# First DFT on rows that are not normalized: factors in its matrix, means as a bias of the copies

## The chip, the cores and the metric

The kernel runs on one core of one Trainium2 chip. The metric is device time of one launch in microseconds; three runs of the kernel before took 1415.65 (median), 1414.65 and 1416.2 us. A profiled execution stands beside them. The engines of the core are named as the profile names them: PE (matrix products; PEld is its loading of stationary matrices), DVE (vector), ACT (scalar engine, with activation functions), POOL (GpSimd) and SP (it issues DMA transfers; ACT and POOL can issue them too). A "q" behind an engine's name (SPq, ACTq) marks its instruction queue, which is where DMA issues show.

## The reference, cut to what matters

An adaptive layer norm, a Fourier block (AFNO) and a gated feed-forward block over 4096 rows of 640 channels:

```python
mod = (_silu(c) @ w_mod).reshape(c.shape[0], 6, 1, -1)
sa, ca, ga, sb, cb, gb = (mod[:, 0], ..., mod[:, 5])
h = _layernorm(x, axis=-1) * (1 + ca) + sa
x = x + ga * _A_ref(h, A_w1, A_b1, A_w2, A_b2)
h = _layernorm(x, axis=-1) * (1 + cb) + sb
x = x + gb * _B_ref(h, B_w_gate, B_w_up, B_w_down)
```

`_A_ref` takes the real FFT over the 4096 rows, multiplies each frequency by two block-diagonal complex layers (4 blocks of 160 channels: `w1`, `b1`, ReLU, then `w2`, `b2`), soft-thresholds at 0.01, and transforms back. `_B_ref` is the gated product `(silu(x w_gate) * (x w_up)) w_down`. Everything is computed in float32, or in pairs of a high and a low part.

## The kernel before, in words

The change touches the first 75 us or so. All of it is one function, `body`, in which each engine's instructions stand in the order in which the code writes them (`tc.manual_schedule()`).

**Stage A.** The 4096 rows are seen as 128 x 32: row n1*32 + n2. Eight tiles `xa0` to `xa7` (in the code `xas[t]`) hold 128 partitions (n1) times 4 values of n2 times 640 channels. For each tile: `ln_stats(t)` takes mean and variance on DVE (BN_STATS, BN_AGGR) and forms on POOL the factor `rs` = (var + eps)^-0.5 and the bias `nm` = -mean * rs; `ln_apply(t)` normalizes the four rows of 640 in place, some on ACT (`Identity` with scale and bias), some on DVE; `dft_a(t)` multiplies by the 128 x 128 DFT matrix `fa`: four products of 512 columns, and a fifth that gathers the last 32 channels of each block of all four rows; `evac_a(t)` copies the five results back over the tile (ACT, for the last two tiles partly DVE); `moves(t)` issues DMA transfers on SP: writes of quarters of the tile to four scratch arrays `s1` in DRAM (`write_s1`), and loads for later (`raws` are the raw weights, `wm1` a block of `w_mod` of 1600 KB).

**Between A and B.** `first_scale`, `remainders` and `columns` make `ca1`, the 1 + ca of the modulation, from `wm1` and silu(c). `weights_high` and `weights_low` split the weights of the first layer, `prep1` (12 jobs), and those of the second, `prep2` (6 jobs), into high and low parts. The second bias `b2` is loaded into one row of a zeroed tile, spread to 128 partitions by three PE products with ones, and copied to `b2t` by ACT. `idle(n)` issues n products whose result nobody uses.

**Stage B and on.** `gs[0]` (called g) holds the spectrum of the first of eight chunks. It is filled by `load_g(0, ...)` from the scratch array s10, which tiles 0 to 5 wrote, and, for tiles 6 and 7, by `move_g`, a copy of 16 rows from the tile straight into four partitions of g (40 KB, four copies per tile). `stage_b` multiplies g by a table; `evac_b` and `evac_r` copy out with the factor `ca1` and split into high (ACT) and low (DVE) parts; `stage_l1` and `stage_l2` are the two layers, for 32 positions (8 chunks times 4 blocks). From there PE works through the rest of the program in a fixed order.

**What orders the DMA issues.** Each transfer that SP or ACT issues carries one of eight semaphores, DMAHW0 to DMAHW7, shared by both engines, and is issued only when the transfer that held the same semaphore before has landed. SP issues in order: an issue that waits holds back all that stand behind it.

Of the kernel before, what the change touches and what calls it, by code (L numbers as in the profile page):

```python
# [6 lines left out]
F32 = mybir.dt.float32  # L7
# [166 lines left out]
def body(tc, x, w1, b1, w2, b2, wg, wu, wd, c, wm, k_fa, k_tb, k_tx, k_bm, k_bx, k_ga, k_ge, k_id, out, dbg=None):  # L174
# [27 lines left out]
    with ExitStack() as top:  # L202
# [35 lines left out]
        with ExitStack() as af:  # L238
# [50 lines left out]
            af.enter_context(tc.manual_schedule())  # L289
            nc.sync.dma_start(fa, k_fa)  # L290
# [45 lines left out]
            stx = ExitStack()  # L336
            xp = stx.enter_context(tc.tile_pool(name="xp", bufs=1, side="right"))
            rp = af.enter_context(tc.tile_pool(name="rp", bufs=1))
            b2t = rp.tile([P, 2, NB, BS], F32, name="b2t")
            with tc.tile_pool(name="sp", bufs=1) as sp:  # L340
                xas = []
                xts = {t: xp.tile([P, 4, D], F32, name=f"xa{t}") for t in (1, 2, 3, 0, 4, 5, 6, 7)}

                def load_x(t):
                    xa = xts[t]
                    if t < 3:
                        for i in range(4):
                            nc.sync.dma_start(xa[:, i, :], xv[:, 4 * t + i, :])
                    else:
                        nc.sync.dma_start(xa, xv[:, 4 * t:4 * t + 4, :])  # L350
                    xas.append(xa)


                def write_s1(t, f):
                    nc.sync.dma_start(s1[f][4 * t:4 * t + 4].rearrange("n r d -> r n d"),
                                      xas[t][(slice(0, 64, 4), slice(64, P, 4), slice(2, P, 4), slice(1, P, 2))[f]])

                for t in range(6):
                    load_x(t)
                wm1 = sp.tile([P, 5, D], F32, name="wm1")  # L360
                stats = {}
                pas = {}
                raws = {}


                def moves(t):
                    if t < 6:
                        write_s1(t, 0)
                    if t < 4:
                        write_s1(t, 1)  # L370
                    if t == 0:
                        load_x(6)
                        nc.sync.dma_start(c5, c)
                    elif t == 1:
                        load_x(7)
                        raws[1] = load_weights(sp, w1, "1")
                    elif t == 2:
                        nc.sync.dma_start(wm1, wm[:, 1])
                    elif t == 3:
                        load_tb(0)  # L380
                        nc.sync.dma_start(b1m, b1[:, 0:8].rearrange("p (r b) -> p r b", r=2))
                        nc.sync.dma_start(b1r, b1[0:64, 8:12])
                        nc.sync.dma_start(b2s[0:1], b2.rearrange("r b o -> (r b o)").unsqueeze(0))
                    elif t == 4:

                        load_g(0, (0, 1))
                        raws[2] = load_weights(rp, w2, "2", (0,))
                    elif t == 5:
                        for f in (2, 3):
                            write_s1(1, f)  # L390
                    elif t == 6:

                        for i in range(4):
                            move_g(0, t, i, (pool, nc.sync)[i // 2])
                        load_g(0, (2,))
                    elif t == 7:
                        for i in range(4):
                            move_g(0, t, i, (pool, nc.sync)[i // 2])


                def ln_stats(t):
                    n = 1 if t < 2 else 4
                    for i in range(0, 4, n):
                        mv, rs = layer_stats(lp, xas[t][:, i:i + n, :], n, f"a{t}_{i}")
                        nm = lp.tile([P, 4], F32, tag="nm", bufs=7, name=f"nm{t}_{i}")
                        pool.tensor_tensor(nm[:, :n], mv[:, :, 0], rs, op=OP.mult)
                        pool.tensor_tensor(nm[:, :n], nm[:, :n], mone[:, :n], op=OP.mult)
                        for k in range(n):
                            stats[t, i + k] = (mv[:, k, 0:1], rs[:, k:k + 1], nm[:, k:k + 1])

                def ln_apply(t):
                    xa = xas[t]
                    for i in range(4):
                        mean, rs, nm = stats[t, i]
                        if i >= (4, 2, 2, 3, 2, 3, 2, 1)[t]:
                            dve.tensor_scalar(xa[:, i, :], xa[:, i, :], mean, rs, op0=OP.subtract, op1=OP.mult)
                        else:
                            act.activation(xa[:, i, :], xa[:, i, :], AF.Identity, bias=nm, scale=rs)


                b2s = sp.tile([P, 2 * NB * BS], F32, name="b2s")
                pool.memset(b2s, 0.0)
                acc0 = sp.tile([P, D], F32, name="acc0")
                wx0 = sp.tile([P, P], F32, name="wx0")

                def first_scale(lo, hi):
                    if lo == 0:
                        dve.tensor_scalar(acc0, wm1[:, 0, :], sc[:, 0:1], None, op0=OP.mult)
                    for k in range(max(lo, 1), hi):
                        dve.scalar_tensor_tensor(acc0, wm1[:, k, :], sc[:, k:k + 1], acc0, op0=OP.mult, op1=OP.add)  # L430

                def dft_a(t):

                    xnr = xas[t].rearrange("p a (b e) -> p a b e", b=NB)
                    for n, i in enumerate((0, 1, 2, 3, 4) if t < 7 else (4, 0, 1, 2, 3)):
                        j = 5 * t + n
                        pa = (bank0(j // 4, [P, 512], f"pa{t}_{i}") if j % 4 == 0
                              else ps.tile([P, 512], F32, tag=f"p{j % 4}", name=f"pa{t}_{i}"))
                        mm(pa, fa, xnr[:, i, :, 0:128] if i < 4 else xnr[:, :, :, 128:160], start=True, stop=True)
                        pas[t, i] = pa  # L440

                def evac_a(t):
                    xa = xas[t]
                    for i in range(5):
                        if t > 5 and i % 2:
                            dve.tensor_copy(xa[:, i, 0:512], pas[t, i])
                        elif i == 4:
                            act.activation(xa[:, :, 512:640], pas[t, i].rearrange("p (a e) -> p a e", a=4), AF.Copy)
                        else:
                            act.activation(xa[:, i, 0:512], pas[t, i], AF.Copy)  # L450

                ln_stats(0)
                ln_stats(1)
                ln_apply(0)
                for t in range(8):
                    if t + 2 < 8:
                        ln_stats(t + 2)
                    if t + 1 < 8:
                        ln_apply(t + 1)
                    dft_a(t)  # L460
                    if t == 6:

                        prep1 = prep_weights(raws[1], w1a, w1b, w1c, True)
                        for job in prep1[:6]:
                            weights_high(*job, pool)
                        first_scale(0, 2)
                    evac_a(t)
                    if t == 6:
                        first_scale(2, 5)
                        remainders(acc0, wx0)  # L470
                    if t == 2:
                        act.activation(sc, c5, AF.Silu)
                    moves(t)

                pm1 = columns(acc0, wx0)
                dve.tensor_scalar(ca1, pm1[:, 0:5], 1.0, None, op0=OP.add)

                pbs2 = []
                for n, w in enumerate((512, 512, 256)):
                    pbs2.append(ps.tile([P, 512], F32, tag="p2" if n else "p1", name=f"pb2_{n}"))  # L480
                    mm(pbs2[n][:, :w], ones, b2s[:, 512 * n:512 * n + w], start=True, stop=True)
                idle(4)
                for job in prep1[6:]:
                    weights_high(*job)
                b2v = b2t.rearrange("p r b o -> p (r b o)")
                for n, w in enumerate((512, 512, 256)):
                    act.activation(b2v[:, 512 * n:512 * n + w], pbs2[n][:, :w], AF.Copy)
                for job in prep1:
                    weights_low(*job)
# [2049 lines left out]
```

## Time and profile before

| what | us |
| --- | --- |
| three runs: median (lowest, highest) | 1415.65 (1414.65, 1416.2) |
| the profiled execution | 1411.32 |
| its span, first to last instruction | 1409.5 |
| PE busy in the span | 1382.5 (98%) |
| first product of stage A starts | 7.98 |
| first product of stage B starts | 55.84 |

The profiled execution is 4.3 us under the median of the runs. Its span is divided by the traces into instructions with a start and a duration; times below are counted from the span's start. In a row of the timeline the first number is the start, the second the time from the start of the first to the end of the last of a merged group, and "x40" the number of instructions in it. A float32 product shows as two instructions. A bracket at the row's end says how long the engine had been idle before, and what it was waiting for.

### The profile page before, as it was taken

To read this page: it belongs to the slowest core of one execution; us is meant where nothing else is said; L and a number is where in the kernel's file an instruction comes from. 1 tells how busy PE (TensorE), PEld (TensorE's weight loads), DVE (VectorE), ACT (ScalarE), POOL (GpSimd) and SP (SyncE) were. 2 spreads that over 40 slices of the span, in tenths; PEclk is the share of its full clock that TensorE was granted. 3 is DMA by queue.
4 is the path that set the end of the run, shared out by engine and by line. 5 is a ranking of instruction groups with operands and counts; after the bars stand their busy time and mean duration, and the time that the engine had idled before them with its cause. 6 is when DMAs were issued, how large, how long until landed. Compare 5 with 4: busy or idle time off the path is not lost. (4 is left out here: it accounts for less than half of the span.)

```text
span 1409.5 us, 23754 instructions
## 1 busy us (share of the span) xinstructions
PE 1382.5 (98%) x8410; PEld 1310.7 (93%) x8410; DVE 1067.8 (76%) x1861; ACT 765.0 (54%) x1542; POOL 604.6 (43%) x683
## 2 busy tenths in 40 slices
PE   6899999999999999999999999999999999999998
PEld 2599999967999889899999999999999999999998
DVE  8889888889888888649787668678678757375644
ACT  6879999755555554436454345546164624262341
POOL 5700200157766594326445534447153624042241
PEclk9999999999999999999999999999999999999999
DMA  9876466675998897898877998696998668956634
GB/s 371 310 244 211 157 196 193 203 232 170 327 353 308 308 335 263 293 368 308 308 225 281 375 330 288 236 326 230 375 330 309 217 218 282 350 194 217 199 115 149
DMA packets 171016, 377.34 MB, mean 268 GB/s; under 512 B 22193, under 2 KB 81649, under 8 KB 168882
## 3 DMA queue, kind: packets, MB, share of 16 engines
q1 hardware_dynamic: 161794, 359.28, 73.6%
q0 software_dynamic: 6800, 13.93, 3.1%
q10 hardware_dynamic: 2304, 2.62, 0.5%
q8 instruction: 66, 1.08, 0.3%
q14 instruction: 52, 0.43, 0.1%
HBM read 269.48 MB, written 96.80 MB: 260 GB/s over the span
## 5 line engine op out<-in xcount | busy, mean ns | idle before, releaser
L1442 DVE TENSOR_TENSOR wb<-r,wb 128x768 fp32r<-128x768 f32 (+3 forms) x170 | 170.4, 1013 | 13.5 <-ACT wb L1435 13.3
L2050 PE MATMUL pw<-h,wt 128*128 128x384 f32 x412 | 139.3, 338 | 0.6 <-ACT s_y L2069 0.6
L2052 PE MATMUL pw<-h,wt 128*128 128x384 f32 x412 | 138.3, 336 | 0.0
L2051 PE MATMUL pw<-h,wt 128*128 128x384 f32 x412 | 138.1, 335 | 0.0
L1435 ACT ACTIVATE wb<-r 128x768 fp32r<-128x768 f32 (+3 forms) x168 | 104.5, 639 | 56.3 <-PE pw L2063 41.7
L2351 PE MATMUL pc<-wq,L 128*128 128x320 f32 x846 | 132.7, 309 | 0.9 <-DMA wq<-wqd 0.9
L2110 POOL TENSOR_TENSOR sg<-s_x,sg 128x384 f32<-128x384 f32 x24 | 30.0, 1250 | 234.5 <-DVE s_x L2076 234.5
L2351 PEld LDWEIGHTS pc<-wq,L 128*128 128x128 f32 x846 | 126.3, 188 | 1.1 <-DVE x L2308 1.1
L2130 DVE TENSOR_TENSOR L<-sg,L 128x384 fp32r<-128x384 f32 x144 | 101.0, 725 | 27.7 <-ACT L L2126 27.2
L2069 ACT ACTIVATE s_x<-pw 128x384 f32<-128x384 f32 x52 | 25.6, 492 | 164.2 <-PE pw L2052 162.3
L2050 PE MATMUL pw<-h,wb 128*128 128x384 f32 x312 | 105.0, 336 | 0.0
L2051 PE MATMUL pw<-h,wb 128*128 128x384 f32 x312 | 104.4, 335 | 0.0
L2052 PE MATMUL pw<-h,wb 128*128 128x384 f32 x312 | 104.4, 335 | 0.0
L2121 POOL TENSOR_TENSOR sg<-sg,sg 128x384 f32<-128x384 f32 x72 | 91.9, 1276 | 23.4 <-DVE L L2130 20.0
L1973 PE MATMUL pg<-ht,wb 128*128 128x512 f32 x260 | 101.8, 392 | 0.0
L2351 PE MATMUL pe<-wq,L 128*128 128x320 f32 x648 | 101.7, 309 | 0.0
L1974 PE MATMUL pg<-ht,wb 128*128 128x512 f32 x260 | 101.3, 390 | 0.0
L1975 PE MATMUL pg<-ht,wb 128*128 128x512 f32 x260 | 101.2, 389 | 0.0
L2267 PE MATMUL pd<-wq,a 128*128 128x320 f32 x632 | 96.8, 310 | 0.0
L2351 PEld LDWEIGHTS pe<-wq,L 128*128 128x128 f32 x648 | 96.6, 188 | 0.0
L2267 PEld LDWEIGHTS pd<-wq,a 128*128 128x128 f32 x632 | 93.5, 188 | 0.5
L772 POOL DMA_DIRECT2D s<-co x28 | 15.7, 559 | 175.9 <-ACT co L771 175.9
(317 smaller groups left out, 3914.1 us busy)
## 6 DMA issues: line engine op xcount, KB each, us to landing
wq<-wqd SPq DMA_DIRECT2D x83, 640.0 KB, 6.1
wt<-td SPq DMA_DIRECT2D x103, 512.0 KB, 5.4
hs<-ho SPq DMA_DIRECT2D x52, 512.0 KB, 5.2
h<-hs SPq DMA_DIRECT2D x32, 768.0 KB, 7.9
td<-wt SPq DMA_DIRECT2D x25, 512.0 KB, 6.3
r<-in_B_w_gate_dram SPq DMA_DIRECT2D x24, 384.0 KB, 4.4
r<-in_B_w_up_dram SPq DMA_DIRECT2D x24, 384.0 KB, 4.3
xx<-tt SPq DMA_DIRECT2D x56, 160.0 KB, 3.3
```

The lines of the kernel that those rows point to most:

```text
L1435: def high(ks, e=slice(0, c), copy=lambda o, i: act.activation(o, i, AF.Copy)):
L1442: dve.tensor_tensor(wbs[t, n][:, 1, ks, e], raw[t, n][:, ks, e], f32(wbs[t, n][:, 0, ks, e]), op=OP.subtract)
L1973: mm(b, wh, hh, start=(kk == 0), stop=False)
L1974: mm(b, wh, hl, start=False, stop=False)
L1975: mm(b, wl, hh, start=False, stop=(kk == 4))
L2050: mm(b, w(0, kp), a[:, kp, 0], start=start and kp == 0, stop=False, skip_group_check=not start)
L2051: mm(b, w(0, kp), a[:, kp, 1], start=False, stop=False, skip_group_check=not start)
L2052: mm(b, w(1, kp), a[:, kp, 0], start=False, stop=kp == 1, skip_group_check=not start)
L2121: pool.tensor_tensor(o, x, y, op=op)
L2130: dve.tensor_tensor(o[:, 1], raws[j], f32(o[:, 0]), op=OP.subtract)
L2267: mm(b[:, :320], l, m, start=start and i == 0, stop=stop and i == len(s) - 1)
L2351: mm(o[:, :320], ls[q][:, x, k], w[:, q, y], start=start and q == 0 and n == 0, stop=q == 1 and n == 2, skip_group_check=not start)
```

## The change

Rows of tiles 1 to 6 are no longer normalized before the DFT. Since the factor `rs` belongs to a partition (n1), over which the DFT sums, it is multiplied into a copy of the DFT matrix: `scaled` makes four matrices `wt` per tile on ACT (128 x 128 each). The means are handled apart: one small product of `fa` with the four columns of `nm` gives the transform of the means (`pa` number 5), `bias_a` copies it to `bt`, and `evac_a` adds it as a bias while it copies. The last 32 channels of each block, which share one product over all four rows, are still normalized in place (`rest`, ACT). Tile 0 is normalized on ACT and tile 7 on DVE, as rows (`ln_row`).

"Moves": tile by tile, `move_g` now brings chunk 0 into g from all eight tiles (32 copies; those of tile 7 with even number on ACT's queue, all others on SP); `write_s1(t, 0)` and `load_g(0, ...)` with data are gone. All eight loads of x stand at the start of SP's queue; c is loaded first on ACT's queue. "Second bias": `b2t` is loaded by one DMA that reads b2 once per partition. "Lower parts": `weights_low` of jobs 6 to 11 of `prep1` stand behind and between the `evac_b`/`evac_r` of the first two blocks. `idle(14)` stands ahead of tile 0, `idle(6)` replaces `idle(4)`. From stage B on each engine's order is that of before.

```diff
+            nc.scalar.dma_start(c5, c)
             nc.sync.dma_start(fa, k_fa)
...
-                for t in range(6):
+                for t in range(8):
                     load_x(t)
+                load_g(0, ())
+                act.activation(sc, c5, AF.Silu)
+                idle(14)
...
                 def moves(t):
-                    if t < 6:
-                        write_s1(t, 0)
+                    for i in range(4):
+                        move_g(0, t, i, nc.scalar if t == 7 and i % 2 == 0 else nc.sync)
                     if t < 4:
                         write_s1(t, 1)
...
                     elif t == 4:
-                        load_g(0, (0, 1))
+                        for f in (2, 3):
+                            write_s1(1, f)
                         raws[2] = load_weights(rp, w2, "2", (0,))
                     elif t == 5:
-                        for f in (2, 3):
-                            write_s1(1, f)
-                    elif t == 6:
-                        for i in range(4):
-                            move_g(0, t, i, (pool, nc.sync)[i // 2])
-                        load_g(0, (2,))
-                    elif t == 7:
-                        for i in range(4):
-                            move_g(0, t, i, (pool, nc.sync)[i // 2])
+                        nc.sync.dma_start(b2t.rearrange("p r b o -> p (r b o)"),
+                                          b2.rearrange("r b o -> (r b o)").unsqueeze(0).to_broadcast([P, 2 * NB * BS]))
...
+                def scaled(t, *rows):
+                    if t not in wts:
+                        wts[t] = sp.tile([P, 4, P], F32, tag="wt", bufs=2, name=f"wt{t}")
+                    for i in rows:
+                        act.activation(wts[t][:, i, :], fa, AF.Copy, scale=stats[t, i][1])
+
+                def rest(t, *rows):
+                    for i in rows:
+                        _, rs, nm = stats[t, i]
+                        v = xas[t][:, i, :].rearrange("p (b e) -> p b e", b=NB)[:, :, 128:160]
+                        act.activation(v, v, AF.Identity, bias=nm, scale=rs)
...
+                    for i in (4, 0, 1, 2, 3) if t == 7 else (0, 1, 2, 3, 4) if t == 0 else (0, 1, 2, 3, 5, 4):
+                        pa = pas[t, i] = bank_a(f"pa{t}_{i}")
+                        if i == 5:
+                            mm(pa[:, 0:4], fa, nms[t], start=True, stop=True)
+                        elif i == 4:
+                            mm(pa, fa, xnr[:, :, :, 128:160], start=True, stop=True)
+                        else:
+                            mm(pa, fa if plain else wts[t][:, i, :], xnr[:, i, :, 0:128], start=True, stop=True)
...
+                for t in range(2, 7):
+                    if t < 6:
+                        ln_stats(t + 2)
+                    scaled(t, 0, 1)
+                    bias_a(t - 1)
+                    rest(t, 0, 1)
...
+                    scaled(t, 2, 3)
+                    evac_a(t - 1, *((2, 3) if t == 2 else (0, 1, 2, 3)))
+                    rest(t, 2, 3)
+                    evac_a(t - 1, 4)
+                    dft_a(t)
+                    moves(t - 1)
+                prep1 = prep_weights(raws[1], w1a, w1b, w1c, True)
+                for job in prep1[:6]:
+                    weights_high(*job, pool)
+                first_scale(0, 1)
+                for i in range(4):
+                    ln_row(7, i)
+                first_scale(1, 2)
+                bias_a(6)
+                evac_a(6, 0, 1, 2, 3, 4)
+                dft_a(7)
+                moves(6)
...
+                evac_a(7, 0, 1, 2, 3, 4)
+                moves(7)
...
-                for n, w in enumerate((512, 512, 256)):
-                    act.activation(b2v[:, 512 * n:512 * n + w], pbs2[n][:, :w], AF.Copy)
-                for job in prep1:
+                for job in prep1[:6]:
                     weights_low(*job)
...
+                weights_low(*prep1[6])
+                evac_b(0, 0)
+                evac_r(0, 0)
+                for job in prep1[7:]:
+                    weights_low(*job)
```

**How instructions stand now: SP.** The names are those of the tiles with a running number behind (`xa3_118` is tile 3, `xa7_123` tile 7), and the brackets name the semaphores that an issue waits for. Before, behind tile 4's write to s10, SP loads parts 0 and 1 of g, and the first copies into g are those of tiles 6 and 7:

```order
L355 DMA s10<-xa4_119 16x4x640 [waits DMAHW2_49,DVE_49,Activation_49]
L311 DMA g0_453<-s10 32x2560 [waits DMAHW3_49]
L311 DMA g0_453<-s10 32x2560 [waits DMAHW4_49]
L253 DMA rm2_456<-in_A_w2_dram 128x1280 [waits DMAHW5_49]
L355 DMA s10<-xa5_120 16x4x640 [waits DMAHW6_49,DVE_49,Activation_49]
```

Now copies of tiles 3 and 4 stand there:

```order
L317 DMA g0_141<-xa3_118 4x4x640 [waits DMAHW5_49,Activation_49]
L317 DMA g0_141<-xa3_118 4x4x640 [waits DMAHW6_49]
L317 DMA g0_141<-xa3_118 4x4x640 [waits DMAHW7_49]
L317 DMA g0_141<-xa3_118 4x4x640 [waits DMAHW1_49]
L416 DMA s11<-xa3_118 16x4x640 [waits DMAHW3_49]
L299 DMA tb0_519<-in_k_tb_dram 128x512 [waits DMAHW4_49]
L444 DMA b1m_81<-in_A_b1_dram 128x8 [waits DMAHW5_49]
L445 DMA b1r_82<-in_A_b1_dram 64x4 [waits DMAHW6_49]
L317 DMA g0_141<-xa4_120 4x4x640 [waits DMAHW7_49,Activation_49]
L317 DMA g0_141<-xa4_120 4x4x640 [waits DMAHW0_49]
L317 DMA g0_141<-xa4_120 4x4x640 [waits DMAHW1_49]
L317 DMA g0_141<-xa4_120 4x4x640 [waits DMAHW2_49]
```

The semaphores go round in turn, 5, 6, 7, but in the fourth and fifth row SP goes on with 1 and 3: 0 and 2 of this round belong to the two transfers of ACT shown next. Behind these rows SP still has, in order, two writes to s1, `rm2`, four copies of tile 5, `b2t`, four of tile 6 and two of tile 7.

**ACT.** Around the end of stage A, before:

```order
L448 ACTIVATE xa6_121<-pa6_4_513 128x4x128 [waits DVE_49,Activation_49]
L450 ACTIVATE xa7_122<-pa7_0_539 128x512 [waits PE_49,Activation_49]
L450 ACTIVATE xa7_122<-pa7_2_543 128x512 [waits DVE_49,PE_49]
L448 ACTIVATE xa7_122<-pa7_4_537 128x4x128 [waits PE_49]
L283 ACTIVATE w1a_92<-rm1_320 128x4x128 [waits DMAHW7_49]
```

Now, with two of the copies of tile 7 behind its last evacuation:

```order
L533 ACTIVATE xa7_123<-pa7_2_640 128x512 [waits PE_49]
L525 ACTIVATE xa7_123<-pa7_4_634 128x4x128 [waits DVE_49,PE_49]
L317 DMA g0_141<-xa7_123 4x4x640 [waits DMAHW0_49,Activation_49]
L317 DMA g0_141<-xa7_123 4x4x640 [waits DMAHW2_49]
L283 ACTIVATE w1a_92<-rm1_394 128x4x128 [waits DMAHW5_49]
```

The two copies are the transfers of this round that hold DMAHW0 and DMAHW2.

**DVE.** Ahead of tile 7's DFT, before:

```order
L416 TENSOR_SCALAR xa6_121<-xa6_121,mv_a6_0_414,rs_a6_0_427 128x640
L416 TENSOR_SCALAR xa7_122<-xa7_122,mv_a7_0_460,rs_a7_0_473 128x640 [waits DVE_49,Pool_49]
L416 TENSOR_SCALAR xa7_122<-xa7_122,mv_a7_0_460,rs_a7_0_473 128x640 [waits DVE_49] x2
L428 TENSOR_SCALAR acc0_141<-wm1_138,sc_67 128x640 [waits DMAHW3_49,Activation_49]
L430 SCALAR_TENSOR_TENSOR acc0_141<-wm1_138,sc_67,acc0_141 128x640 [waits DVE_49]
```

And now:

```order
L495 TENSOR_SCALAR acc0_159<-wm1_158,sc_67 128x640 [waits DMAHW4_49,Activation_49]
L476 TENSOR_SCALAR xa7_123<-xa7_123,mv_a7_0_524,rs_a7_0_531 128x640 [waits Pool_49]
L476 TENSOR_SCALAR xa7_123<-xa7_123,mv_a7_0_524,rs_a7_0_531 128x640
L476 TENSOR_SCALAR xa7_123<-xa7_123,mv_a7_2_535,rs_a7_2_542 128x640 [waits DVE_49,Pool_49]
L476 TENSOR_SCALAR xa7_123<-xa7_123,mv_a7_2_535,rs_a7_2_542 128x640 [waits DVE_49]
L497 SCALAR_TENSOR_TENSOR acc0_159<-wm1_158,sc_67,acc0_159 128x640 [waits DVE_49]
```

The first multiplication with `wm1`, which waits for that load, moved from behind the rows of tile 7 to ahead of them.

More of the change, by code (lines that the diff above doesn't have):

```diff
@@ L624, in evac_rh @@
                 if b == 0:
[L625 removed]
+                    rzs[ch] = lp.tile([P, NB, 258], F32R, tag="rz", bufs=2, name=f"rz{ch}")
                     if ch == CE:
@@ new lines, in mod_sum @@
+            def mod_sum(m, hf=0):
+                if m == 0:
+                    pm = columns(acc, wx)
+                    dve.tensor_scalar(sa4, pm[:, 0:5], float(S), None, op0=OP.mult)
+                elif m == 2:
+                    pm = ps.tile([P, 512], F32, tag="p3", name=f"pm{m}_{hf}")
+                    mm(pm[:, :320], ones, acc[:, 320 * hf:320 * hf + 320], start=True, stop=True)
+                    act.activation(gab[:, 320 * hf:320 * hf + 320], pm[:, :320], AF.Copy)
+                else:
+                    pm = ps.tile([P, 512], F32, tag="p3", name=f"pm{m}")
+                    for t in range(5):
+                        mm(pm[:, t:t + 1], acc[:, 128 * t:128 * t + 128], ones[:, 0:1], start=True, stop=True)
+                    if m == 3:
+                        dve.tensor_copy(sb1, pm[:, 0:5])
+                    else:
+                        dve.tensor_scalar(cb1, pm[:, 0:5], 1.0, None, op0=OP.add)
@@ new lines, in body @@
+            weights_rest(3)
+            weights_high(*prep2[5], pool)
+            weights_rest(5)
+            mods = {26: [(load_e,)]}
+            sums = {}
+            for i, m in enumerate((0, 2, 3, 4)):
+                for k in range(5):
+                    mods.setdefault(3 + 6 * i + k, []).append((mod_load, m, k))
+                    mods.setdefault(5 + 6 * i + k, []).append((mod_add, m, k))
+                sums.setdefault(11 + 6 * i if m < 4 else LAST, []).append((mod_sum, m, 1))
+                if m == 2:
+                    sums.setdefault(10 + 6 * i, []).append((mod_sum, m, 0))
```

393 lines of the change are left out of this document (182 added, 211 removed).

## The prediction

> **What bounds the kernel now.** I read the page first (busy shares, the span in slices), then the waits of PE by stretch, then the timeline of the head engine by engine.
>
> ```profile
> PE 1382.5 (98%) x8410; PEld 1310.7 (93%) x8410; DVE 1067.8 (76%) x1861; ACT 765.0 (54%) x1542; POOL 604.6 (43%) x683
> PE   6899999999999999999999999999999999999998
> ...
> PE py L1688 <- DMA gt<-in_k_ga_dram: 1.5, 1, 1.5
> ```
>
> PE is busy all through except in the first slices, and from 75 us to the end its longest single wait is 1.5 us (last row). So from 75 us on PE bounds, and the order there is that of before: when the head ends later by d, the end is later by d. The question is when stage B starts, and how long PE needs from there until it is dense.
>
> ```profile
> 7.98 4.64 PE L439 MATMUL pa<-xa,fa 128*128 128x512 f32 x5 [7.98 <-ACT xa L418]
> 19.60 4.82 PE L439 MATMUL pa<-xa,fa 128*128 128x512 f32 x10
> 31.56 17.74 PE L439 MATMUL pa<-xa,fa 128*128 128x512 f32 x40 [1.81 <-ACT xa L418]
> 48.48 0.60 ACT L450 ACTIVATE xa<-pa 128x512 f32<-128x512 f32 x1 [1.06 <-PE pa L439]
> 49.34 0.60 ACT L448 ACTIVATE xa<-pa 128x512 f32<-128x512 f32 x1 [0.26 <-PE pa L439]
> 50.76 1.20 SPq L316 DMA_DIRECT2D g<-xa  x2
> 55.84 2.92 PE L600 MATMUL pb<-tb,g 128*128 128x128 f32 x24 [1.43 <-DMA g<-xa]
> ```
>
> Rows 3 to 7 are the chain at the end of the head: products of stage A until 49.30, the last evacuations until 49.94, copies into g until 51.96, stage B at 55.84 after a wait for g. In stage A PE is nearly full: 40 records in 17.74 us is .427 each for the second of every pair (a product is two records, .86 us). DVE and ACT, which the change relieves, therefore hold PE by little: the gap of 1.81 us in row 3, the .71 us ahead of tile 1, and the start at 7.98. The gain to be had is a few us of 49; against it stands what the change does to SP's queue.
>
> **The change part by part.** *Work removed.* DVE normalizes 4 rows instead of 13 and ACT 4 instead of 19:
>
> ```profile
> 40.53 1.95 DVE L416 TENSOR_SCALAR xa<-xa,mv_a,rs_a 128x640 f32<-128x640 f32 x3 [0.93 <-POOL rs_a L198]
> 34.61 2.55 ACT L418 ACTIVATE xa<-xa,nm,rs_a 128x640 f32<-128x640 f32 x3
> 51.39 0.30 ACT L283 ACTIVATE w1a<-rm 128x128 fp32r<-128x128 f32 x1
> 51.59 0.30 ACT L283 ACTIVATE w1b<-rm 128x128 fp32r<-128x128 f32 x1
> 51.13 2.40 PE L481 MATMUL pb<-b2s,ones 128*128 128x512 f32 x6
> 53.13 0.87 ACT L487 ACTIVATE b2t<-pb 128x512 f32<-128x512 f32 x2 [0.26 <-PE pb L481]
> 29.19 1.28 ACT L472 ACT_TABLE_LOAD   x1
> ```
>
> On DVE 9 x .65 (1.95/3) = 5.9 us go; on ACT 15 x .85 (2.55/3) = 12.8 us, and 1.28 for a table load. ACT gets 24 `scaled`, 24 `rest` and 6 `bias_a`: the 128x128 copies start .20 apart, so 54 x .20 = 10.8. The second bias loses 2.40 on PE, .87 and another half of it on ACT; its broadcast DMA adds 640 KB. The six products with `nm` are at most .20 each. PE gets 20 records of `idle(14)` and `idle(6)` together, ahead of tile 0 and behind tile 7, where it idles before anyway. All of this I cost at nothing, gains and losses, because tile 7's products and stage B will be set by other things, below. If that cover fails, the lighter engines could give back at most the 1.81 + .71 us above.
>
> *wm1 is issued later.* SP's queue now begins with all loads of x, 8 x 1.31 MB, so all have to come in at the rate seen:
>
> ```profile
> 0.00:10.00 10.00, 2.02 (x3) 0.94 (x4) 4.82 (x21) 3.12 (x3) 4.64 (x16) 1.00 0.77 246
> 10.00:20.00 10.00, 9.29 (x18) 3.63 (x17) 9.79 (x31) 6.49 (x10) 7.89 (x25) 1.00 1.04 424
> 20.00:30.00 10.00, 9.65 (x22) 3.56 (x20) 10.00 (x34) 9.67 (x16) 3.88 (x8) 1.00 1.02 419
> fa<-in_k_fa_dram SPq DMA_DIRECT2D x1, 64.0 KB, 1.9
> SPq L348 <- DMA xa<-in_A_x_dram: 1.6, 2, 1.0
> SPq L350 <- DMA xa<-in_A_x_dram: 1.4, 3, 0.5
> wm<-in_w_mod_dram SPq DMA_DIRECT2D x1, 1600.0 KB, 11.0
> ```
>
> (Last two numbers of the windows: DMA share and GB/s.) 10.49 MB are 2.46 in the first 10 us, 4.24 in the next, and the remaining 3.79 at 419 GB/s: 29.0, plus 1.9 for a landing = 31.0 for tile 7. Rows 5 and 6 show the semaphore rule at work before: SP stood 3.0 us for earlier loads of x when it issued loads into fresh tiles. SP's third copy of tile 1 has the semaphore of tile 7's load, hence goes out at 31.0. Behind it stand ten issues ahead of `wm1`:
>
> ```profile
> 25.79 0.43 SPq L253 DMA_DIRECT2D rm<-in_A_w_dram  x1
> 26.26 0.48 SPq L253 DMA_DIRECT2D rr<-in_A_w_dram  x1
> 29.20 1.18 SPq L355 DMA_DIRECT2D s<-xa  x2
> 30.43 0.58 SPq L378 DMA_DIRECT2D wm<-in_w_mod_dram  x1
> 42.40 0.97 DVE L428 TENSOR_SCALAR acc<-wm,sc 128x640 f32<-128x640 f32 x1
> ```
>
> That is 6 copies at .60 (1.20/2 above), 2 writes at .59, .43 and .48: 5.7, with the gaps 5.9, so `wm1` is issued at 36.9 instead of 30.43. It lands between 42.6 (its bytes and what is queued, 3.3 MB from 32.9 on at .42 MB/us, plus 1.9) and 47.9 (36.9 and the 11.0 of before); I take 44.0, nearer to the first, since the loads of x that filled its 11.0 us are done. Before, `first_scale` waited for this load behind tile 7's rows; now it stands ahead of them. So tile 7's rows begin at 44.0 + .97 and end 4 x .65 later: its first product starts at 47.6. Before, its ten records began about 45.0 (49.30 less ten of .427). Tile 6 is done near 42, so PE idles some 5.5 us ahead of tile 7.
>
> *Cold products.* Rows 1 and 2 of the head show two speeds of the same record: five started in 4.6 us after the idle 7.98 us, ten in 4.8 us later on. After the gap of 1.81 us there is no slow stretch. The new gap of 5.5 us lies between the two; 5.5 is nearer to 7.98, so I take the slow speed for five records: 5 x .42 = 2.1 us. (The windows show a clock of 1.00 in both stretches, so only the spacing tells.) [...] Product 2 of tile 7 is then done at 47.6 + 2.1 + 4 x .86 = 53.2, and ACT's two last evacuations of .60 end at 54.5.
>
> *SP waits for ACT.* This is the main term. ACT's two copies of tile 7 hold DMAHW0 and DMAHW2 of the round in which SP issues tile 3's copies; SP's second copy of tile 4 is the next user of DMAHW0, and stands there until ACT's copy has landed. ACT can't issue it before tile 7 is evacuated, 54.6.
>
> ```profile
> out_dram<-x ACTq DMA_DIRECT2D x12, 160.0 KB, 1.8
> g<-xa POOLq DMA_DIRECT2D x4, 40.0 KB, 5.0
> 52.01 0.44 SPq L492 DMA_DIRECT2D rr<-in_A_w_dram  x1
> ```
>
> A copy of 40 KB issued by ACT lands between 1.8 us (ACT's own writes of 160 KB at the end of the program) and 5.0 (POOL's copies of the same 40 KB in the head); with less traffic than in the head I take 2.5: 57.1. Only then SP issues, in a row: 3 copies of tile 4, two writes, `rm2`, 4 copies of tile 5, `b2t`, 4 of tile 6, 2 of tile 7. That is 13 copies at .60, 2 writes at .59, and .44 twice: 9.9; with gaps, 17 x .61 = 10.4, of which the last issue takes .6. It starts at 66.9, lands 1.8 to 5.0 later, and I take 3.5, the middle: g is whole at 70.4. Stage B waits for all of g: 70.4 instead of 55.84, +14.6. The 16 issues ahead of the last are pure SP time, as long as no landing in the round is later than its eighth successor's issue (8 x .61 = 4.9 us); landings of 5 us just fit.
>
> *Lower parts, and the start of stage B.* Jobs 6 to 11 now stand behind the first residues on DVE:
>
> ```profile
> 54.53 0.69 DVE L286 SCALAR_TENSOR_TENSOR w1b<-rm,w1b 128x512 fp32r<-128x512 f32 x1
> ...
> 56.14 0.28 DVE L286 SCALAR_TENSOR_TENSOR w1c<-rr,w1c 128x128 fp32r<-128x128 f32 x1
> 57.73 0.75 DVE L608 SCALAR_TENSOR_TENSOR z<-pb,ca,z 128x512 fp32r<-128x512 f32 x1 [1.31 <-ACT z L607]
> ```
>
> Five of them are 1.9 us (54.53 to 56.42). Before, they lay ahead of g, with 1.31 us of idle behind them; now DVE has nothing to do from about 51 to 70, and then has them on the path of `z`. Most of 1.9 is lost, up to all of it. PE comes from 14 us of idling to stage B; its first twelve products (24 records in 2.92 us, a third of them of the next group) start at the slow speed, at most 1.5 us more. Together 1.6 to 3.4, taken as 2.6: the parts overlap, as a slow PE gives DVE time.
>
> *Sum.* 14.6 + 2.6 = +17.2. Against the profiled execution of 1411.32 (span 1409.5) that is 1428.5. The median of the runs, 1415.65, lies 4.3 higher, for all of the program; the difference is added to it: 1432.9.
>
> [...] The table of DMA issues gives 6.7 us for the quarter writes of 160 KB and 5.0 for copies of 40 KB, at a full queue, so size alone can't be told from waiting. [...]
>
> **The rivals.**
> - *Copies on a quarter of the engines.* If a 40 KB copy moves at a quarter of the 424 GB/s of the windows, it takes .39 us instead of .10; if each of the last 6 waits for the one ahead, g comes 6 x .29 = 1.7 us later: 1434.6. The 5.0 us of POOL's copies speak for it, the full queue at that time against it.
> - *No slow products.* If 5.5 us of idling doesn't slow PE, 2.1 fall away at tile 7, and at stage B 1.0: 1432.9 - 3.1 = 1429.8. For it: a clock of 1.00 in every window.
> - *SP is not held by ACT's copy.* If SP goes on at 46 with tile 4 and only `wm1` is late, stage B starts about 2.6 us later (tile 7 at 47.6 instead of 45.0), and the lower parts and slow products cost up to 2.6: 1415.65 + 5.2 = 1420.8. Against it: SP did stand for landings in the two rows of waits.
> - *The other side: no wait for a semaphore's earlier holder binds at all.* Then `wm1` keeps its place behind the same bytes and lands near 40.5, tile 7 starts at 40.5 + .97 + 2.6 = 44.1 (-.9), the copies from SP land in 3.5 instead of POOL's 5.0 (-1.5), and the lower parts cost 1.6: -.8, 1414.8, within what can't be told from no change. It decides if SP's second copy of tile 4 goes out before 46 and `wm1` before 33. The same two rows speak against it.
>
> **How the numbers follow.** The forecast with slow products in both places .50; a quarter of the engines .18; no slow products .20; SP not held .04; no semaphore binds .03; something else .05, spread. About .2% (2.8 us) is what a measurement of this kernel can tell from no change. All but the fourth rival and a part of the rest are slower: slower .94, the same .04, faster .02. The time is the forecast's, 1432.9. Its unknowns are the landing of `wm1` (-1.4, +3.9), of ACT's copy (-.7, +2.5), of the last copy (-1.7, +1.5) and the start of stage B (-1.0, +.8). Added as independent, the lower side is 2.6 and the upper 5; with the rival without slow products at 1429.8 and its own spread the range reaches down to 1426.5, with the quarter of the engines up to 1438.5.
>
> **What would show it.** In the trace after: SP idle from about 46 to 57 ahead of the second copy of tile 4, released by a copy into g; then 17 issues without a gap; `wm1` landing near 44, with DVE idle ahead of the first `acc`; PE idle for 5 to 6 us ahead of tile 7's first product and for 14 us ahead of stage B, and after both gaps records at .85 instead of .43; stage B's first product near 70; from 90 us on the same rows as before, 17 us later. It is wrong if SP issues tile 4's copies as soon as tile 4 is evacuated, or if stage B starts before 62.

## The result, and the profile after

The changed kernel took 1437.97 us (median of 4 runs, 1435.35 to 1441.57), the kernel before 1415.93 (4 runs): 1.0155 of it, with a 95% interval of 1.0128 to 1.0181. It is 22 us slower; the forecast was 17.2, with a range that ended at 1438.5. The profiled execution is the lowest of the four, 1435.35, with a span of 1433.5.

The page first (busy shares and the span in slices), then the two waits of PE and of SP that carry the head, by the view of waits between 40 and 90 us (PE) and 40 and 57 us (SP):

```profile
PE 1391.0 (97%) x8448; PEld 1320.1 (92%) x8448; DVE 1059.4 (74%) x1851; ACT 769.9 (54%) x1578; POOL 597.8 (42%) x690
PE   8499999999999989999999999999999999999998
```

```profile
PE pb L351 <- DMA rr<-in_A_w_dram: 17.0, 1, 17.0
PE pa L513 <- DVE xa L476: 1.9, 1, 1.9
...
PE pl L720 <- DVE w1c L286: 1.3, 1, 1.3
```

```profile
SPq L317 <- DMA g<-xa: 8.7, 2, 8.1
SPq L299 <- DMA wm<-in_w_mod_dram: 3.5, 1, 3.5
```

PE is busy 8.5 us longer than before, most of it the added idle products and slow records; the loss is one hole, 17.0 us ahead of stage B, in the second slice. (Its wait is put down to `rr`, but stage B reads g and tb only: by the semaphore events of the trace the last copy into g landed at 72.60, .09 us ahead.) SP stands 8.1 us for the landing of a copy into g, and ahead of that 3.5 for `wm1`. The timeline of the head of PE, of DVE where `wm1` arrives, of ACT at the end of stage A, and of SP:

```profile
45.15 1.13 PE L513 MATMUL pa<-xa,fa 128*128 128x512 f32 x2 [0.67 <-ACT xa L488]
48.22 1.13 PE L513 MATMUL pa<-xa,fa 128*128 128x512 f32 x2 [1.94 <-DVE xa L476]
49.18 3.60 PE L515 MATMUL pa<-xa,fa 128*128 128x512 f32 x8
72.69 5.19 PE L351 MATMUL pb<-tb,g 128*128 128x128 f32 x24 [17.00 <-DMA rr<-in_A_w_dram]
89.57 0.60 PE L770 MATMUL pc<-w2a,h 128*128 128x320 f32 x3
```

```profile
45.52 0.55 DVE L495 TENSOR_SCALAR acc<-wm,sc 128x640 f32<-128x640 f32 x1 [9.86 <-DMA wm<-in_w_mod_dram]
```

```profile
53.44 1.75 ACTq L317 DMA_DIRECT2D g<-xa  x2
```

```profile
36.23 0.58 SPq L441 DMA_DIRECT2D wm<-in_w_mod_dram  x1
...
46.97 9.29 SPq L317 DMA_DIRECT2D g<-xa  x2
55.70 0.56 SPq L317 DMA_DIRECT2D g<-xa  x1
...
63.05 5.09 SPq L317 DMA_DIRECT2D g<-xa  x6
```

Read from the right end: ACT's copies of tile 7 go out at 53.44, as the last evacuation ends. SP's copies of tile 4 begin at 46.97; the second of them starts at 55.70, when ACT's first copy has landed (55.69 by its semaphore events). From there SP issues with short waits only until its last copy into g, the sixth of the row at 63.05, and stage B starts at 72.69. The same place in the kernel before is

```profile
70.42 0.61 PE L711 MATMUL pc<-w2a,h 128*128 128x320 f32 x3
```

so that at the second layer's first products the changed kernel is 89.57 - 70.42 = 19.15 us late, of which 16.85 were there when stage B began. At PE's last product it is 23.7, and 24.0 by the spans (1433.5 - 1409.5). The 4.6 us in which the lateness grows from 19.15 to 23.7 come at one late wait, for `gt`, and behind it, told with the experiments.

### The profile page after: what moved, and what is told of

Its sections match the earlier page's. It is cut to its first block, busy times and chain, and to the rows that moved or that the text cites. A ratio compares the mean times of both kernels' runs of the same rounds, so it can differ in the third digit from the quotient of the medians.

```text
span 1433.5 us, 23911 instructions
## 1 busy us (share of the span) xinstructions
PE 1391.0 (97%) x8448; PEld 1320.1 (92%) x8448; DVE 1059.4 (74%) x1851; ACT 769.9 (54%) x1578; POOL 597.8 (42%) x690
```

## The experiments

Each kernel was timed in five rounds beside the kernel before; ratios are to that one. The changed kernel, timed once more in this way, stands first.

**Once more.**

> The changed kernel once more, on the chip of the runs beside it: its time against the kernel before was 1.0155 (1.0128 to 1.0181), and that is expected again.

Measured 1.0167 (1.0145 to 1.0190), 1435.81 against 1413.88 us. Its profile shows what varies from execution to execution of one and the same kernel:

```profile
49.47 1.12 PE L513 MATMUL pa<-xa,fa 128*128 128x512 f32 x2 [2.92 <-DVE xa L476]
50.43 5.29 PE L515 MATMUL pa<-xa,fa 128*128 128x512 f32 x8
```

```profile
PE py L1731 <- DMA gt<-in_k_ga_dram: 1.6, 1, 1.6
```

Here the gap ahead of tile 7 was 2.92 us, and eight records took 5.29 instead of 3.60: the slow products that the profile above does not have. Stage B began at 75.23. Then again the wait for `gt`, 1.6 here (view of waits from 500 to 560 us), was 3.7 in the first profile. The two profiled executions lose nearly the same by their last product, 22.6 us here and 23.7 in the first, but at different places: here 21.7 of it was there at the second layer's first products.

**SP held by ACT's copy.** All copies of tile 7 on SP:

```diff
-                        move_g(0, t, i, nc.scalar if t == 7 and i % 2 == 0 else nc.sync)
+                        move_g(0, t, i, nc.sync)
```

> The changed kernel with all four copies of tile 7 on SP, so that no copy of ACT holds a semaphore that SP needs earlier. Theory (SP is held by ACT's copy): SP issues tile 4's second copy near 47 instead of 55.70, the issues up to tile 7's last copy run from 45.8 on, 20 of them at .65 us, the last near 59, and stage B starts at 62 instead of 72.69; the time falls by 10 to 11 us, to 1427. Rival (the late wm1 and the rows of tile 7 behind it set the end, the hold only fills the time): stage B moves by less than 2 us and the time stays at 1436 to 1438.

Measured 1.0109 (1.0083 to 1.0136); stage B at 65.27, 7.4 us earlier than in the first profile of the changed kernel.

```profile
46.35 0.57 SPq L445 DMA_DIRECT2D b1r<-in_A_b_dram  x1
47.03 2.38 SPq L317 DMA_DIRECT2D g<-xa  x4
...
55.63 6.28 SPq L317 DMA_DIRECT2D g<-xa  x8
```

All four copies of tile 4 go out from 47.03 on: the hold is gone, and it was ACT's copy. What is left ahead of them is the wait of 3.5 us for `wm1`, up to the first row shown. In time the ratio falls by .0046 to .0058, 6.5 to 8 us, where 10 to 11 were expected, and stage B begins 3 us later than expected, since SP took 14.9 us for the 20 issues from 47.03 on (.75 each), with waits of .7, .5 and .6 us for `rm2`, b2t and ACT's evacuation among them, and tile 7 fell into slow records:

```profile
49.14 2.07 PE L513 MATMUL pa<-xa,fa 128*128 128x512 f32 x2 [2.33 <-DVE xa L476]
51.01 5.39 PE L515 MATMUL pa<-xa,fa 128*128 128x512 f32 x8
...
65.27 4.34 PE L351 MATMUL pb<-tb,g 128*128 128x128 f32 x24 [6.42 <-DMA g<-xa]
```

A window of that profile has the clock beside it (after the busy times of PE, its loads, DVE, ACT and POOL; then DMA share and GB/s):

```profile
48.00:50.00 2.00, 0.86 (x1) 0.50 (x2) 2.00 (x5) 0.66 (x2) 0.00 (x0) 0.50 0.23 75
```

PE had waited .67 and 2.33 us within 4 us, and the granted clock went to .50.

**Rows of tile 7 first.** On DVE the first multiplication by `wm1` behind them:

```diff
-                first_scale(0, 1)
                 for i in range(4):
                     ln_row(7, i)
-                first_scale(1, 2)
+                first_scale(0, 2)
```

> The changed kernel with the first multiplication by wm1 behind the rows of tile 7 on DVE, as in the kernel before. Theory (wm1 delays tile 7, whose evacuation releases SP): tile 7's first product starts at 46.4, right behind tile 6, instead of 48.22, and everything behind it, SP's issues too, is 1.8 us earlier: 1436.2. Rival (the evacuations of tile 6 on ACT keep tile 7 where it is): no change, 1438.

Measured 1.0141 (1.0113 to 1.0170). Tile 7's products follow tile 6's without a gap, and stage B begins 2.7 us earlier, at 70.02:

```profile
45.06 1.98 PE L513 MATMUL pa<-xa,fa 128*128 128x512 f32 x4 [0.67 <-ACT xa L488]
```

So `wm1`, and its new place on DVE, did delay tile 7, by 2 to 3 us. In time the difference to the changed kernel lies within the intervals; the trace shows it, the ratio alone doesn't.

**PE kept at work.** `idle(60)`, then `idle(74)`, instead of `idle(6)` behind tile 7:

> The changed kernel with idle(60) in place of idle(6): PE multiplies ones until about 70 us and idles under 3 us ahead of stage B instead of 17. Theory (the slow start of stage B is PE's clock after idling): its first 24 records take 2.9 us instead of 5.19, and the time falls by 2.3 us, to 1435.7. Rival (the first products are slow because g and tb are still being written, or for another reason in the data): the 24 records keep 5.2 us and the time stays at 1438.

> The changed kernel with idle(74) in place of idle(6): at the .114 us for each record that the run with idle(60) showed, PE multiplies ones until 70.9 and stops 2 us ahead of stage B instead of 17 (in the run with idle(60) it stopped 4.7 ahead, and stage B stayed slow). Theory (the slow start of stage B is PE's clock after idling): the first 24 records of stage B take 2.9 us instead of 5.2, and the time falls by 2.3 us against the changed kernel. Rival (another reason in the data): they keep 5.2 us, the time is the same.

Measured 1.0144 (1.0117 to 1.0171) and 1.0145 (1.0127 to 1.0163). The first stopped too early, since a record took .114 us and not the .13 I had counted on:

```profile
54.73 13.64 PE L335 MATMUL pz<-ones 128*128 128x128 f32 x120
73.08 5.20 PE L351 MATMUL pb<-tb,g 128*128 128x128 f32 x24 [4.71 <-DMA s<-xa]
```

The second kept PE at work until 1.60 us ahead of stage B:

```profile
75.86 2.92 PE L351 MATMUL pb<-tb,g 128*128 128x128 f32 x24 [1.60 <-DMA g<-xa]
```

After 17.0 us of idling the 24 records took 5.19 us, after 4.71 us 5.20, after 1.60 us 2.92: here idling sets their speed, and the price is 2.3 us. It varies: 6.42 and 5.86 us of idling in the runs with all copies on SP and with the order put right gave 4.34 and 4.55. The expected fall of 2.3 us in time isn't resolved, as the intervals of both ratios overlap with those of the changed kernel, and stage B began no earlier. In the changed kernel's windows the clock is .50 ahead of that place, and 1.00 again from 78 us on:

```profile
64.00:72.00 8.00, 0.00 (x0) 0.00 (x0) 0.00 (x0) 1.36 (x2) 5.46 (x4) 0.50 0.66 206
...
78.00:80.00 2.00, 1.88 (x14) 1.51 (x13) 1.97 (x3) 1.94 (x5) 1.92 (x2) 1.00 1.09 324
```

**A late head alone.** The kernel before with `idle(68)` in place of `idle(4)`:

> The kernel before with idle(68) in place of idle(4): stage B starts at 71.3 instead of 55.84, with PE warm, and nothing else is changed. Theory (behind the head PE bounds, a shift of d in the head is d at the end): 1415.9 + 15.5 = 1431.4. Rival (a late head also lengthens the later waits of PE, which in the changed kernel grew by 4.6 us at 344 and 530 us): 1434 to 1436.

Measured 1.0076 (1.0050 to 1.0103), 1424.59 against 1411.5: 13.1 us. The idle products took .113 us a record here too, so stage B began at 68.46, 12.6 us late and not 15.5. A shift of 12.6 gave 13.1 in the medians, which looks like one to one. The profile shows that it isn't, step by step. At the second layer the lateness is 10.15 us (80.57 - 70.42), as PE's waits there for DVE (1.1 us for `r` and .7 for `z` in the kernel before) are gone:

```profile
80.57 0.60 PE L711 MATMUL pc<-w2a,h 128*128 128x320 f32 x3
```

From there it goes through whole up to the wait for `gt` (10.1 ahead of it, at 518.87 in this profile), and that wait was 1.7 us, against 1.5 before. At the end of this execution it is 15.0 (1424.5 - 1409.5): smaller waits behind 700 us added the rest. So the theory holds from the second layer to the late waits, and those vary by as much as the rival's price. That the medians agree with 12.6 is in part luck.

**The wait for gt.** POOL issues tile 0's copies, so that its loads of `gt` carry the same semaphores as before:

```diff
-                        move_g(0, t, i, nc.scalar if t == 7 and i % 2 == 0 else nc.sync)
+                        move_g(0, t, i, nc.scalar if t == 7 and i % 2 == 0 else pool if t == 0 else nc.sync)
```

> The changed kernel with the four copies of tile 0 issued by POOL instead of SP: POOL issues as many transfers in the head as in the kernel before. It tells what lengthens PE's later wait for gt (1.5 us before, 3.7 in the changed kernel, and again after idling a slow PE). Theory (gt is loaded by POOL, whose semaphores go round, and the head's four missing issues moved it to another place in the round): the wait is 1.5 us again, no slow records at 530 us, and the time falls by 3 to 4 us. Rival (gt lands late because of the traffic of SP's queue at that place): it stays at 3 to 4 us; stage B, which hangs on SP's later issues, stays at 72 to 73 by both.

Measured 1.0147 (1.0129 to 1.0166). In its profile PE waits 3.4 us for `gt`: the turn of the semaphores is not the cause. What that wait costs the first profile of the changed kernel is read from it and from the kernel before, at the same instruction:

```profile
508.62 0.38 PE L1688 MATMUL py<-chh,gt 128*128 128x320 f32 x1 [1.51 <-DMA gt<-in_k_ga_dram]
```

```profile
530.05 0.38 PE L1731 MATMUL py<-chh,gt 128*128 128x320 f32 x1 [3.74 <-DMA gt<-in_k_ga_dram]
```

The lateness is 21.43 us here (530.05 - 508.62), 2.2 of it from the wait (1.51 to 3.74), so 19.2 ahead of it, as at the second layer. Behind it slow records follow, at a granted clock of .96 between 500 and 540 us against 1.00 before, and smaller waits, up to 23.7. The long wait isn't forced by the change: an execution of the changed kernel without it exists (1.6 us, above), and of the two runs below that keep the transfers of the kernel before, one has it (3.7) and one doesn't (1.1). Between its issue and PE's use of it `gt` took 4.2 us in the kernel before, 5.9 here and 4.3 in the second profile; why, was not settled.

**The order put right.** Five moves, the new DFT kept:

```diff
+                wm1 = sp.tile([P, 5, D], F32, name="wm1")
+                nc.sync.dma_start(wm1, wm[:, 1])
                 load_g(0, ())
...
-                        move_g(0, t, i, nc.scalar if t == 7 and i % 2 == 0 else nc.sync)
+                        move_g(0, t, i, nc.sync)
...
-                        for f in (2, 3):
-                            write_s1(1, f)
...
-                first_scale(0, 1)
...
-                first_scale(1, 2)
+                first_scale(0, 2)
...
-                for job in prep1[:6]:
+                for job in prep1:
                     weights_low(*job)
```

(The load of `wm1` at its old place goes away; the writes of tile 1 and the load of b2t go behind the copies.)

> The changed kernel with five moves of issues and order: wm1 loaded right behind the x loads; all copies of tile 7 on SP; the first multiplication by wm1 behind tile 7's rows; the two writes of tile 1 and the load of b2t behind the copies into g; all lower parts ahead of stage B. Theory (the order of the issues and of DVE costs the time, not the new DFT): wm1 lands at 34, tile 7's products start at 46.4, SP's issues run from 34 on, 32 of them at .65 us, the last copy starts near 55, and stage B starts at 58 to 59; with the waits behind it as in the changed kernel the time is 1.003 to 1.006 of the kernel before. Rival (ACT, full in stage A since it scales the matrices, would keep stage B beyond 62 whatever the order): 1.009 or more.

Measured 1.0070 (1.0050 to 1.0090), where the theory had 1.003 to 1.006 and the rival 1.009 or more: about 1 percentage point comes back, 12 us between the medians of the same rounds (1435.81 and 1424.18). Tile 7 starts right behind tile 6 and SP's last copies go out one behind the other:

```profile
50.49 7.28 SPq L317 DMA_DIRECT2D g<-xa  x12
```

```profile
59.87 4.55 PE L351 MATMUL pb<-tb,g 128*128 128x128 f32 x24 [5.86 <-DMA g<-xa]
```

Stage B begins 2.1 us after the last copy ends its issue (57.77); it is SP's 32 issues, .61 each, that still end last, 4.0 us behind the kernel before. The slow records come on top (4.55 us instead of 2.92), and then waits of PE for POOL's parts of the second layer's weights (1.5, 1.2 and .8 us).

**The new DFT alone**, and with DVE helping. The loads, writes, copies, second bias, lower parts and the place of `first_scale` are those of the kernel before; then DVE takes over

```diff
-                        elif t == 6 and i % 2:
+                        elif t in (4, 5, 6) and i % 2:
                             dve.tensor_scalar(xa[:, i, 0:512], pas[t, i], bts[t][:, i:i + 1], None, op0=OP.add)
...
+                        if t == 6:
+                            dve.tensor_scalar(v, v, stats[t, i][0], rs, op0=OP.subtract, op1=OP.mult)
```

> The new DFT alone: factors in the matrix, means as a bias, and idle(14) at the start, but with the loads, writes, copies, second bias, lower parts and the place of the first multiplication by wm1 of the kernel before. Theory (ACT, at 5.54 us for a tile in the changed kernel, paces stage A, and PE's 4.7 is not reached): tile 7's first product at 46.4 against 45.0 before, stage B at 57.3 against 55.84, the time 1.001 of the kernel before. Rival (the rows taken off DVE and ACT shorten stage A by the 2.5 us that PE waited there): 0.998.

> As the run with the new DFT alone, but DVE, idle from 36 us on, copies out two of the four rows of tiles 4 and 5 (ACT's .57 us each) and normalizes the last 32 channels of tile 6 (1.54 us of ACT). Theory (ACT paces stage A): the tiles 5 to 7 follow at 4.7 us instead of 5.54, tile 7 starts near 44.5, stage B at 55.3, the time 0.999 to 1.000 of the kernel before, and 1.5 to 2 us under the run with the new DFT alone. Rival (PE or DVE paces it): no difference between the two.

Measured 1.0026 (1.0011 to 1.0040) and 1.0022 (1.0007 to 1.0036). (Both keep `idle(14)` and the early load of c.) The forecasts were 1.001, and .999 to 1.000: both times came out slower than expected. The first rival, .998, is outside the interval. In time the DFT alone costs 3 to 4 us; the other 18 or so of the 22 belong to the moves, the second bias, the lower parts and the place of `wm1`. In the head it costs less: at the second layer's first products (70.42 before) the two runs are at 71.53 and 69.91, 1.1 us late and .5 early. The rest came behind the head, in the first of the two profiles mostly at the wait for `gt`. ACT paces it: in the profile of the new DFT alone the tiles follow at 5.54 us (40.06 to 45.60), with DVE's help at 4.5:

```profile
40.06 1.12 PE L526 MATMUL pa<-xa,fa 128*128 128x512 f32 x2 [0.67 <-ACT xa L499]
45.60 1.98 PE L526 MATMUL pa<-xa,fa 128*128 128x512 f32 x4 [0.67 <-ACT xa L499]
...
55.77 2.92 PE L351 MATMUL pb<-tb,g 128*128 128x128 f32 x24 [0.41 <-DMA g<-xa]
```

```profile
38.63 1.10 PE L529 MATMUL pa<-xa,fa 128*128 128x512 f32 x2
43.15 1.96 PE L529 MATMUL pa<-xa,fa 128*128 128x512 f32 x4
...
50.47 4.09 PE L603 MATMUL pb<-b2s,ones 128*128 128x512 f32 x6
55.29 2.84 PE L351 MATMUL pb<-tb,g 128*128 128x128 f32 x24
```

Stage B is at 55.77 and 55.29, as before: 2.4 us of stage A saved are lost again, in a wait of .79 us for `acc` and in the products of the second bias (4.09 us for six records that took 2.40 before; the granted clock was .50 from 52 to 54 us). The two ratios can't be told apart. None of the kernels beats the one before.

## Why the prediction was right

The direction, the mechanism and the size came out: 22.0 against 17.2 us, inside the range, near its upper end. That the size came out so near is in part luck: 2.1 us for slow products of tile 7 that did not come made up for part of what the row of issues and the last landing lacked, and behind the head the time varies by several us. By the steps of the sum, with the first profile of the changed kernel:

| step | predicted | measured |
| --- | --- | --- |
| `wm1` issued; DVE's first use of it | 36.9; 44.0 | 36.23; 45.52 |
| PE idle ahead of tile 7, first product | 5.5, 47.6 | 1.94, 48.22 |
| slow records in tile 7 | 2.1 | 0 (1.7 in the second profile) |
| ACT's copy issued; SP goes on | 54.6; 57.1 | 53.44; 55.70 |
| start of the first to start of the last of SP's 17 issues | 9.8 | 11.9 |
| start of the last issue to stage B | 3.5 | 5.1 |
| stage B later by | 14.6 | 16.85 |
| from there to the second layer | 2.6 | 2.3 |
| behind the head | 0 | 4.6 (about 1 in the second profile) |

- *SP is held by ACT's copy* was right and is shown by the run with all copies on SP: the hold goes with it, and 7.4 us of stage B's lateness.
- *The row of issues* was mis-sized, +2.1 us. I counted 16 x .61 and let landings of 5 us "just fit". `rm2`, issued at 58.84, held its semaphore longer: the issue that needed it next waited 1.3 us for it (65.63, `rm2` landed at 65.61). Another .5 is one long issue, 1.08 us, at 59.55. The term was sized from issue times, where a transfer of 640 KB among them ought to have been counted by its landing.
- *The last landing* was mis-sized, +1.6 us: 5.1 instead of 3.5. The semaphore events of the trace show why. The load of b2t, issued at 62.47, made 12 of the 16 updates of its landing by 66.65 and the last four by 68.98; behind it the six last copies landed one after the other, at 69.39, 69.86, 70.29, 71.12, 71.82 and 72.60. So they had queued behind b2t, and on few engines (.26 of the 16 busy from 66 to 68 us). In the kernel with b2t behind the copies, stage B follows the end of the last issue after 2.1 us, against 4.55 here. The rival of copies on a quarter of the engines, given .18, was right in its mechanism: its quarter was an assumption that no row of before gave, and the slices after show 85 to 108 GB/s against 364 to 421 (below). Its price, 1.7 us, is near what the landing lacked, but it acts together with the load by b2t, and no run parts the two.
- *Slow products at tile 7* rested on a gap of 5.5 us. It was 1.94: tile 6 ended at 46.28 and not at 42. That is the step that failed outright, "all of this I cost at nothing": ACT's new instructions were counted at .20 us each. They take .30 for a scaling and .39 for a `rest` (two scalings .59 and two rests .77 apart in the profile), 16.6 us for these two alone in place of 10.8 for all. The prediction left out, too, that an evacuation with a bias is dearer: four take 2.28 us where four without took 1.90. Per tile that is 1.18 + 1.54 + 2.28, and .53 for the fifth evacuation and `bias_a`: 5.53, the pace of 5.54 us at which the tiles follow. ACT was busy 10.00 of 10 us from 20 to 30 and from 30 to 40. Before, tiles 4 to 7 took 17.74 us, 4.4 each. It cost little here since tile 7 waited for `wm1` anyway; with tile 6 done at 42, that wait would only have been 4 us longer. It does set the floor: in the run with the rows first, tile 7 still starts near 46.
- *wm1* was right as a wait (1.5 us later than taken, inside its bounds) and the run with the rows first shows its share, 2.7 us.
- *Stage B and the lower parts*: 2.3 us for slow records, by the run with `idle(74)`, and 1.28 for `w1c`, the last lower part, of which a part comes back by 88 us.
- *Behind the head* the sum had nothing. From the second layer on the shift goes through whole (19.15 there, 19.2 ahead of the wait for `gt`), as in the late head alone; the 4.6 us of the first profile are late waits that vary from one execution to the next.

## What to carry to other kernels

Where two engines issue transfers on one ring of semaphores, look at which transfer holds the semaphore of each issue, not at the queue alone: one copy issued late by ACT stopped SP for 8.1 us, though SP's data were ready. A row of small transfers costs its number of issues (.6 to .75 us each on SP here), and moving data early by many copies pays only while SP has nothing else to issue: 32 copies instead of 8 and three loads put SP at the end of the head, and stage B 4.0 us later even with the order put right. When an engine is relieved, its replacement work has to be priced by that shape's own rows: 15 long instructions (.85 us each) gave way to 54 short ones (.30 for a scaling, .39 for a `rest`), and ACT became the pace of stage A, 5.54 us a tile.

## What the runs showed of the hardware

- The copies of 40 KB ran at about a quarter of the bandwidth. Between 65.4 and 69.0 us, when copies and the last quarter of b2t were left in flight, 85 to 108 GB/s were moved, against 364 to 421 in the slices that the loads of 640 KB ahead of it fill (view of transfers of the changed kernel, 55 to 73 us, in slices of .45 us):

```profile
DMA  1020112259999999579999942222222789998999
GB/s 57 11 80 0 57 51 74 74 216 375 421 375 370 262 233 302 137 284 364 376 410 398 324 103 91 108 102 102 108 85 108 165 245 353 262 211 245 302 427 370
```

  About .2 of the engines is busy (first row, in tenths); the view of windows gives .26 of the 16 for 66 to 68 us. By the semaphore events of the trace, b2t's landing is 16 updates of its semaphore and a copy's is four (those of the last copy at 71.85, 71.89, 72.04 and 72.60), behind one update 1 to 1.5 us after the start of its issue; I read that, with the .26, as four engines for a copy. At a quarter of the 424 GB/s of the windows before, a copy of 40 KB would take .39 us, an estimate; in the changed kernel tile 5's four copies, which landed behind `rm2` (65.61), came .36 to .41 us apart (66.25, 66.61, 67.01 and 67.42). That is less than the .6 of an issue, so here it cost only where copies piled up behind a load.
- The prediction had left the gap that slows PE between 1.81 and 7.98 us. It is shorter than I had thought, and not one value: ahead of tile 7, gaps of 2.33 (all copies on SP), 2.59 (`idle(74)`) and 2.92 us (once more) brought slow records, 1.94 (the first profile) and 2.40 did not. The last is from the run with `idle(60)`:

```profile
48.84 1.12 PE L513 MATMUL pa<-xa,fa 128*128 128x512 f32 x2 [2.40 <-DVE xa L476]
49.80 3.60 PE L515 MATMUL pa<-xa,fa 128*128 128x512 f32 x8
```

  So one and the same kernel lost 1.7 us at tile 7 in one execution (gap 2.92) and nothing in another (1.94). What sets the border was not shown.
